# A two-block transformer layer on one core: the columns 1+ca as wide products, one pass for their stationary, and a new order of all operations

## The chip, the core and the metric

The kernel runs on one core of a Trainium2 chip. The core has five engines that run side by side, each in the order of its own instruction list: TensorE (PE, matrix products; PEld is its loading of the stationary operand), VectorE (DVE), ScalarE (ACT), GpSimd (POOL) and SyncE (SP), which here only issues DMAs. They wait for each other through semaphores. Products land in PSUM, eight banks of 128 x 512 floats; everything else lives in SBUF, which has 128 partitions.

The metric is the device time of one execution in microseconds (us). Of several executions the median counts.

## The reference

A layer with conditioning: six vectors of 512 numbers are made from `c`, and each of two blocks gets a shift, a scale and a gate.

```python
mod = (_silu(c) @ w_mod).reshape(c.shape[0], 6, 1, -1)
sa, ca, ga, sb, cb, gb = (mod[:, 0], mod[:, 1], mod[:, 2], mod[:, 3], mod[:, 4], mod[:, 5])
h = _layernorm(x, axis=-1) * (1 + ca) + sa
x = x + ga * _A_ref(h, A_wqkv, A_wo)                          # linear attention, 32 heads of 16
h = _layernorm(x, axis=-1) * (1 + cb) + sb
x = x + gb * _B_ref(h, B_w_in, B_w_sp, B_b_sp, B_w_out)       # gated MLP, mixing over positions
```

Block A: q, k, v = h @ wqkv; with phi(t) = (t+1 for t > 0, else exp(t)) + 1e-6 it sums phi(k) v and phi(k) over all positions for each head, multiplies by phi(q), divides, and applies wo. Block B: z = gelu(h @ w_in), split in two halves of 688; the second half is normalized and mixed over the positions by the 2048 x 2048 matrix w_sp, plus b_sp; the product of the halves goes through w_out. x is 2048 x 512. All is in 32-bit floats.

## The kernel before

The 2048 positions are 16 tiles of 128 rows, t = 0 to 15; the 512 features are four chunks of 128, kc = 0 to 3. Large products are made from operands split in a high part that is rounded for a faster matmul mode and a low part that holds the rest (`hi_lo`, `mm3`: three matmuls hi x hi, hi x lo, lo x hi, lines 110 to 112).

The program has two parts. Part one, in stages:

- **Head** (0 to about 38 us). The vector 1+ca is needed as a column for each chunk, because the layer norm's scale is folded into the weights. `silu` makes `sil` from `c`. `col_mm` (`cm`, line 196) multiplies each 128 x 128 block of w_mod[1], as stationary operand, by one column of `sil` and adds up into PSUM tile `pcol1`, 128 x 4. `col_end` (`ce1`, line 208) copies it to SBUF with 1 added. `mean_col` (`mc`, line 328) makes from it and from a tile `inv` filled with 1/512 a stationary `cbr` of four blocks, each with equal columns (1+ca)/512, in one ACT pass for each block. `mean_mm` (`mr`, line 334) multiplies `cbr` by w_k (j = 1) or w_q (j = 0): every row of the result `wm` is the mean to be taken out. `w_mid` (`wf`, line 338, on DVE) makes the folded weight w * (1+ca) - mean, `w_hi` (`qh`, ACT) and `w_lo` (`qd` on DVE, `qg` on POOL, line 345) split it into `wk` and `wq`. `load_m`, `load_wk` and `load_w` load w_mod, w_k and w_q; `dummy` (`du`, line 174) makes pairs of matmuls of ones that no one reads.
- **k, q and G** (to about 160 us). For each tile: the transposed x is split (`th`, `tl`, tile `ht`), products k (`kk`, `km`) and q (`qm`), phi on ACT and DVE, and `gm`, which adds phi(k)^T x into two PSUM tiles `g`.
- **The attention's small products** (to about 184 us): `kv` (tile `pkv`), mask and split into `kvh` (`kx`), then the four products with the gated w_o (`mm`, tile `pm`, one for each chunk; they share two PSUM tiles) and their splitting (`me`, tile `m`).
- **Output of block A and z** (to about 365 us). For each tile: q transposed (on PE, tile `tpp`, or by a DMA), the product with `m` (`wo`, tile `po`), x1, layer norm, transposing of h2 (tile `ht` again), the two z products with w_in (`z0`, `z1`, line 652: 24 matmuls each), gelu, and stores to DRAM. The last modulation row is made at the end (`mV`, `mS`, `mB`; tile `mod`).

Part two mixes over positions (`pp` for the first four row blocks, tile `Pq`; `pr` for the others by a scheme with fewer products, tile `P`, both line 930) and multiplies by w_out (`wm`, tile `pout`).

The order of the work is written out by hand: `ORDER` and `ORDER3` are lists of about 850 and 750 words, each an operation and its tile, in which every engine's instructions are recorded, and `SLOTS` says for each kind of buffer which of its places the next tile takes. A tile that takes a place must wait until the last reader of the tile before is done. All DMAs go through SP's one queue, in the order of the words. Line numbers here are those of the profile.

Of the kernel before, what the change touches and what calls it, by code (L numbers as in the profile page):

```python
# [26 lines left out]
def block_kernel(ctx: ExitStack, tc: tile.TileContext, x, x_t, w_qkv, w_o, w_in, w_sp, b_sp, w_out,  # L27
# [163 lines left out]
    def col_mm(m, kc):  # L191
        if m not in CP:
            CP[m] = ps("t", [P, KC], f"pcol{m}")
        for i in range(KC):
# [1 line left out]
            mm(CP[m][:, i:i + 1], RAW["mod", m, kc // 2][:, kc % 2, i * P:(i + 1) * P], sil[:, kc:kc + 1],
               start=n == 1, stop=n == KC * KC, skip_group_check=True)
# [8 lines left out]
    def col_end(key):  # L206
        COL[key] = const.tile([P, KC], F32, name=f"col{key}")
        nc.scalar.activation(COL[key], CP[key], AF.Copy, bias=1.0 if key == 1 else 0.0)
# [564 lines left out]
    def hx_lo(t):  # L773
# [21 lines left out]
        bh1 cr0 ce0 bp0 ly5 th5 lx2 s12 kr1 bh2 lx4 km2 kr2 qd0,1 by0 by1 by2 by3 bp3 qd0,3 qm0 bx1 bp1 tl5
        bh0 bp2 bb1 be1 bl0 ka0 qm1 qm2 qr0 qr1 lM2 ba1 ba2 ba3 lx5 s15 k20 bx0 km5 k40 bb0 s14 kh0 kl0 bl2
        ka2 gm0 be0 ly4 q12 th3 bh4 tl3 km3 lx3 qm3 lw2,0 k15 th4 s13 q22 q42 tl4 km4 qm4 bl1 kr3 ka1 mV2,0
        mV2,1 q13 k21 ly10 th10 bh3 bl3 k41 ks0 ks1 lw2,1 vh2 k22 k42 kh1 kl1 mS2 k25 kh2 bl4 k45 vh3 ly6 th6
        k14 k24 ks2 q14 q24 gm1 kl2 vh0 ly11 tl10 tl6 ly8 th11 th8 mB2 q44 lo0 lx6 s16 qm5 q15 ka3 k23 tl8 vl3
        ly9 km6 k16 k43 qm6 ks3 th9 tl9 tl11 lx9 s19 lx8 kh3 gm2 kl3 qa1 k44 ks4 q25 km8 s18 q16 bh9 kh4 gm3  # L800
        kl4 gm4 ly7 th7 tl7 bh6 vh1 lx7 ks5 k26 q45 km7 qm7 wg0 wx0 bl6 k46 lo1 wg2 bh8 bl8 kh6 kl6 q26 k18
        lx11 s17 q21 bl9 q46 kh5 ly15 th15 tl15 km9 bh5 wx2 ks6 bl5 k17 q41 q17 km11 ly12 k27 kl5 k47 k28 k48
        kh7 ly13 vl0 kl7 vl1 ks7 vl2 k19 th12 gm5 s111 lx15 km10 gm6 ly14 lx10 qa0 q27 tl12 ks8 wy0 qm10 s115
        q23 q43 bh7 kh8 vp0 q47 k111 s110 qm11 k29 kl8 k49 kh9 k110 k210 bl7 th13 q110 k211 k410 kh10 wg3 wx3
# [363 lines left out]
```

## Time and profile before

| what | value |
|---|---|
| median of 3 runs | 656.33 us (650.57 to 656.46) |
| the profiled execution: time, span of its instructions | 656.31 us, 654.2 us |
| PE busy | 629.8 us, 96% of the span |
| DVE busy | 506.2 us, 77% |
| ACT busy | 334.6 us, 51% |
| POOL busy | 226.6 us, 35% |
| 16 DMA engines, hardware queue | 53.5% |
| costliest matmuls | z, x768: 126.8 us; P, x576: 95.4 us; Pq, x384: 61.5 us |

Two other parts of the page show the span in 40 slices of 16.4 us and the chain of work that ended last. In a slice row each digit is a tenth of the slice's time.

```profile
PE   9999989999889899979999999999999999999998
DVE  0789999998779689864884579799698789884762
DMA  8235431344234555863473586642745767689862
PE 44%; DVE 15%; ACT 7%; issue 4%; DMA 3%; POOL 2%; SPq 0%; DVEq 0%; ACTq 0%; POOLq 0%
```

PE is nearly full everywhere. DVE is nearly full in slices 3 to 9, which are the k, q and G stage. DMA is fullest in the first slice. The chain's row adds up to 75% of the span, since its first piece starts at 161 us.

### The profile page before, as it was taken

To read this page: it belongs to the slowest core of one execution; us is meant where nothing else is said; L and a number is where in the kernel's file an instruction comes from. 1 tells how busy PE (TensorE), PEld (TensorE's weight loads), DVE (VectorE), ACT (ScalarE), POOL (GpSimd) and SP (SyncE) were. 2 spreads that over 40 slices of the span, in tenths; PEclk is the share of its full clock that TensorE was granted. 3 is DMA by queue.
4 is the path that set the end of the run, shared out by engine and by line. 5 is a ranking of instruction groups with operands and counts; after the bars stand their busy time and mean duration, and the time that the engine had idled before them with its cause. 6 is when DMAs were issued, how large, how long until landed. Compare 5 with 4: busy or idle time off the path is not lost.

```text
span 654.2 us, 9565 instructions
## 1 busy us (share of the span) xinstructions
PE 629.8 (96%) x3407; PEld 568.7 (87%) x3407; DVE 506.2 (77%) x910; ACT 334.6 (51%) x563; POOL 226.6 (35%) x186
## 2 busy tenths in 40 slices
PE   9999989999889899979999999999999999999998
PEld 9587777777778889879899999999999999998886
DVE  0789999998779689864884579799698789884762
ACT  1577775646446865457452564445444345443430
POOL 0562425625674566633524521140312221110000
PEclk9999999999999999989999999999999999999999
DMA  8235431344234555863473586642745767689862
GB/s 285 105 111 176 129 96 34 113 124 142 61 110 121 116 135 143 199 156 100 142 228 124 174 314 235 150 146 85 215 99 169 209 173 223 173 314 251 261 233 89
DMA packets 91310, 105.74 MB, mean 162 GB/s; under 512 B 57120, under 2 KB 57632, under 8 KB 91264
## 3 DMA queue, kind: packets, MB, share of 16 engines
q1 hardware_dynamic: 91264, 105.15, 53.5%
q8 instruction: 26, 0.43, 0.3%
q14 instruction: 20, 0.16, 0.1%
HBM read 66.07 MB, written 25.95 MB: 141 GB/s over the span
## 4 chain that ended last, share of the span: by engine, by line
PE 44%; DVE 15%; ACT 7%; issue 4%; DMA 3%; POOL 2%; SPq 0%; DVEq 0%; ACTq 0%; POOLq 0%
PE P L930 18%; PE Pq L930 9%; PE z L652 3%; PE pout L111 3%; PE pout L112 3%; PE pout L110 3%; DVE xpp L279 2%; DVE bst L250 2%; DVE xph L279 1%; POOL mv L255 1%; DVE h L262 1%; DMA wor<-in_w_out 1%; DVE ht L299 1%; DVE xr L628 1%; DVE h L261 1%
## 5 line engine op out<-in xcount | busy, mean ns | idle before, releaser
L652 PE MATMUL z<-win,ht 128*128 128x344 f32 x768 | 126.8, 324 | 7.3 <-DVE ht L299 2.8
L652 PEld LDWEIGHTS z<-win,ht 128*128 128x128 f32 x768 | 122.5, 191 | 11.4 <-DVE ht L299 3.5
L930 PE MATMUL P<-z,f 128*128 128x344 f32 x576 | 95.4, 320 | 1.1 <-DVE f L920 1.0
L930 PEld LDWEIGHTS P<-z,f 128*128 128x128 f32 x576 | 91.3, 188 | 1.7 <-DVE f L920 1.6
L920 POOL TENSOR_TENSOR f<-raw_wsp,f 128x512 fp32r<-128x512 f32 x24 | 37.5, 1575 | 122.9 <-ACT f L917 98.6
L255 POOL TENSOR_TENSOR mv<-ve,mhalf 128x1 f32<-128x1 f32 x48 | 37.5, 798 | 74.5 <-DVE ve L254 57.6
L930 PE MATMUL Pq<-z,wsp 128*128 128x344 f32 x384 | 61.5, 321 | 1.3 <-ACT mod L241 1.3
L930 PEld LDWEIGHTS Pq<-z,wsp 128*128 128x128 f32 x384 | 61.0, 188 | 1.6 <-ACT mod L241 1.5
L917 ACT ACTIVATE f<-sa 128x512 fp32r<-128x512 f32 x36 | 22.7, 630 | 50.2 <-DVE sa L907 12.5
L917 ACT ACTIVATE f<-raw_wsp 128x512 fp32r<-128x512 f32 x48 | 29.1, 625 | 21.4 <-PE P L930 9.4
L688 POOL TENSOR_TENSOR z<-zz,z 128x688 fp32r<-128x688 f32 x16 | 29.1, 1834 | 26.0 <-ACT z L685 26.0
L920 DVE TENSOR_TENSOR f<-sa,f 128x512 fp32r<-128x512 f32 x36 | 27.2, 758 | 9.1 <-ACT f L917 9.0
L111 PE MATMUL pout<-wout,ut 128*128 128x512 f32 (+1 forms) x85 | 32.5, 382 | 0.3 <-DVE wout L1050 0.3
L112 PE MATMUL pout<-wout,ut 128*128 128x512 f32 (+1 forms) x85 | 32.3, 380 | 0.0
L110 PE MATMUL pout<-wout,ut 128*128 128x512 f32 (+1 forms) x85 | 32.2, 379 | 0.0
L269 ACT COPY uca<-us 128x768 uint16<-128x768 uint16 x32 | 25.0, 828 | 13.8 <-DVE us L985 10.3
L472 POOL TENSOR_TENSOR pksum<-pksum,tk 128x512 f32<-128x512 f32 x15 | 22.7, 1511 | 26.3 <-DVE tk L444 19.5
L110 PE MATMUL kp<-wk,ht 128*128 128x512 f32 x64 | 26.0, 407 | 3.2 <-DVE tk L423 3.2
L1019 ACT ACTIVATE ut<-ur 128x384 fp32r<-128x384 f32 x32 | 15.5, 519 | 26.4 <-DMA ur<-ud 11.5
L269 ACT COPY xph<-h 128x512 uint16<-128x512 uint16 x28 | 15.9, 615 | 22.4 <-DVE h L262 17.8
L111 PE MATMUL kp<-wk,ht 128*128 128x512 f32 x64 | 25.4, 397 | 1.0 <-DVE wk L345 1.0
L112 PE MATMUL po<-m,pt 128*128 128x512 f32 x64 | 25.3, 396 | 0.6 <-POOL pt L299 0.6
(257 smaller groups left out, 1553.6 us busy)
## 6 DMA issues: line engine op xcount, KB each, us to landing
raw_wsp<-in_w_sp SPq DMA_DIRECT2D x32, 512.0 KB, 5.0
ud<-uca SPq DMA_DIRECT2D x16, 384.0 KB, 3.7
ur<-ud SPq DMA_DIRECT2D x16, 384.0 KB, 4.9
z1d<-z SPq DMA_DIRECT2D x16, 344.0 KB, 2.4
zd<-zz SPq DMA_DIRECT2D x16, 344.0 KB, 2.8
z1r<-z1d SPq DMA_DIRECT2D x16, 344.0 KB, 3.7
xt<-in_x_t SPq DMA_DIRECT2D x16, 256.0 KB, 2.8
x<-in_x SPq DMA_DIRECT2D x16, 256.0 KB, 2.8
```

The costliest lines, as they stand in the source:

```text
L110: mm(o, a_hi, b_hi, start=first, stop=False, **kw)
L111: mm(o, a_hi, b_lo, start=False, stop=False, **kw)
L112: mm(o, a_lo, b_hi, start=False, stop=last, **kw)
L255: nc.gpsimd.tensor_tensor(mv[:, 1:2], ve, mhalf, op=OP.pow)
L269: nc.scalar.copy(pl[:, h], v[:, :, h])
L279: copy(o[:, :, h], plt[:, h * n:(h + 1) * n].rearrange("p a b -> p (a b)"))
L472: nc.gpsimd.tensor_add(pksum, pksum, PK[t])
L652: mm(p[:, b, :HB], a[:, i, kc], win[h][:, j, kc, b * HB:(b + 1) * HB], start=kc == 0 and k == 0, stop=kc == KC - 1 and k == 2)
L688: nc.gpsimd.tensor_sub(Z2[t][:, 1], ZZ[t], f(Z2[t][:, 0]))
L917: nc.scalar.activation(SF[p, h, k][:, 0], s_src(p, h, k), AF.Copy)
L920: eng.tensor_sub(SF[p, h, k][:, 1], s_src(p, h, k), f(SF[p, h, k][:, 0]))
L930: mm(B[key][:, :HB], a[:, x_], b[:, y_], start=i == 1, stop=i == n)
```

## The change

Four things change.

1. `col_mm` multiplies by 128 equal columns of `sil` (a broadcast of one column) instead of one; the PSUM tile `pcol1` becomes 128 x 4 x 128, one bank.
2. `mean_col` makes the whole stationary `cbr` from that bank in one ACT pass, p/512 + 1/512. The tile `inv` and its fill go. `ce1` takes column 0 of each block and is no longer needed ahead of `cbr`.
3. On SP, w_k's fourth chunk is loaded before the second tile of x_t, and w_q's two loads stand together.
4. `ORDER`, `ORDER3` and `SLOTS` are new throughout. Six of eleven `du` and three of four `mc` words are gone; all other words are the same, in another order.

```diff
-    inv = sb("md", [P, P], F32R, "inv")
-    nc.gpsimd.memset(f(inv), 1.0 / D)
...
     def col_mm(m, kc):
         if m not in CP:
-            CP[m] = ps("t", [P, KC], f"pcol{m}")
+            CP[m] = ps("t", [P, KC, P], f"pcol{m}")
         for i in range(KC):
             n = NCOL[m] = NCOL.get(m, 0) + 1
-            mm(CP[m][:, i:i + 1], RAW["mod", m, kc // 2][:, kc % 2, i * P:(i + 1) * P], sil[:, kc:kc + 1],
-               start=n == 1, stop=n == KC * KC, skip_group_check=True)
+            mm(CP[m][:, i], RAW["mod", m, kc // 2][:, kc % 2, i * P:(i + 1) * P],
+               sil[:, kc:kc + 1].to_broadcast([P, P]), start=n == 1, stop=n == KC * KC, skip_group_check=True)
...
-        nc.scalar.activation(COL[key], CP[key], AF.Copy, bias=1.0 if key == 1 else 0.0)
+        p = CP[key][:, :, 0] if key == 1 else CP[key]
+        nc.scalar.activation(COL[key], p, AF.Copy, bias=1.0 if key == 1 else 0.0)
...
-    def mean_col(kc):
-        if "c" not in WC:
-            WC["c"] = sb("tb", [P, KC, P], F32, "cbr")
-        nc.scalar.activation(WC["c"][:, kc], f(inv), AF.Copy, scale=COL[1][:, kc:kc + 1])
+    def mean_col():
+        WC["c"] = sb("tb", [P, KC, P], F32, "cbr")
+        nc.scalar.activation(WC["c"], CP[1], AF.Copy, scale=1.0 / D, bias=1.0 / D)
...
-        lm1,0 si du1 du2 du3 du4 du5 cm1,0 lm1,1 du6 cm1,1 lm1,2 du7 cm1,2 lm1,3 lk1 lk0 du8 cm1,3 ce1 mc0 ly1
+        si lm1,0 du1 du2 du3 du4 cm1,0 lm1,1 cm1,1 lm1,2 cm1,2 lm1,3 cm1,3 mc lk0 lk1 ly1 th1 tl1 lk2 lk3 du5
```

Three places of the new order, as the recorded instruction lists show them (line, operation, output<-inputs, size; numbers in names only tell tiles apart).

The head, on PE, before:

```order
L174 MATMUL warm<-ones 128x128 x10
L196 MATMUL pcol_187<-sil,raw_mod_0_170 128x1 x4
L174 MATMUL warm<-ones 128x128 x2
L196 MATMUL pcol_187<-sil,raw_mod_0_170 128x1 x4
L174 MATMUL warm<-ones 128x128 x2
L196 MATMUL pcol_187<-sil,raw_mod_1_199 128x1 x4
```

And now:

```order
L172 MATMUL warm<-ones 128x128 x8
L194 MATMUL pcol_183<-sil,raw_mod_0_173 128x128 x8
L194 MATMUL pcol_183<-sil,raw_mod_1_193 128x128 x8
L172 MATMUL warm<-ones 128x128 x2
L332 MATMUL wm_219<-raw_qkv_0_206,cbr 128x512 x2
```

The dummies between the columns are gone, and the sixteen column products stand together. The same place on SP, before:

```order
L156 DMA raw_qkv_0_208<-in_w_qkv 128x512 x2
L150 DMA xt_221<-in_x_t 128x512
L156 DMA raw_qkv_1_226<-in_w_qkv 128x512
L150 DMA xt_231<-in_x_t 128x512
L156 DMA raw_qkv_1_226<-in_w_qkv 128x512
L144 DMA raw_qkv_0_250<-in_w_qkv 128x1024
L156 DMA raw_mod_0_255<-in_w_mod 128x512
L144 DMA raw_qkv_1_257<-in_w_qkv 128x1024
```

And now:

```order
L154 DMA raw_qkv_0_206<-in_w_qkv 128x512 x2
L148 DMA xt_209<-in_x_t 128x512
L154 DMA raw_qkv_1_214<-in_w_qkv 128x512 x2
L148 DMA xt_221<-in_x_t 128x512
L154 DMA raw_mod_0_226<-in_w_mod 128x512
L142 DMA raw_qkv_0_230<-in_w_qkv 128x1024
L142 DMA raw_qkv_1_232<-in_w_qkv 128x1024
```

The fourth chunk of w_k moved ahead of the second x_t tile, and the two loads of w_q no longer have a load of w_mod between them.

The products with the gated w_o, on PE, before; of each product only the first of its three rows is shown:

```order
L306 MATMUL tpp_1742<-ident,pq_473 128x128 x4
...
L110 MATMUL pm_0_1753<-wog_920,kvh 128x512
...
L110 MATMUL pm_0_1753<-wog_1311,kvh 128x512
...
L110 MATMUL pm_2_1769<-wog_977,kvh 128x512
...
L110 MATMUL pm_2_1769<-wog_1163,kvh 128x512
```

And now:

```order
L305 MATMUL tpp_1700<-ident,pq_430 128x128 x4
...
L110 MATMUL pm_0_1716<-wog_1061,kvh 128x512
...
L110 MATMUL pm_2_1722<-wog_1267,kvh 128x512
...
L110 MATMUL qp_1729<-wq_161,ht_1017 128x512
...
L110 MATMUL pm_0_1716<-wog_1224,kvh 128x512
...
L110 MATMUL pm_2_1722<-wog_1232,kvh 128x512
```

The q product of tile 14, twelve matmuls, stood ahead of all four; it now stands between the first pair, one in each PSUM tile, and the second.

The border of the two programs, on PE, before:

```order
L652 MATMUL z_14_3664<-win_1440,ht_14_3460 128x344 x24
L238 MATMUL pmod_3701<-yh_3595,ones 128x512
L239 MATMUL pmod_3701<-yl_3596,ones 128x512
L930 MATMUL Pq_0_3767<-z_0_2574,wsp_0_3350 128x344 x3
L930 MATMUL Pq_1_3771<-z_0_2574,wsp_0_3350 128x344 x3
```

And now:

```order
L237 MATMUL pmod_3658<-yh_3590,ones 128x512
L238 MATMUL pmod_3658<-yl_3591,ones 128x512
L650 MATMUL z_15_3663<-win_1707,ht_15_3475 128x344 x24
L928 MATMUL Pq_0_3749<-z_0_2534,wsp_0_3621 128x344 x3
L928 MATMUL Pq_1_3753<-z_0_2534,wsp_0_3621 128x344 x3
```

The last modulation row's products moved ahead of the last z product, and the first mixing product is that of row block 1, whose PSUM banks are others than those of block 0.

More of the change, by code (lines that the diff above doesn't have):

```diff
@@ L795, in block_kernel @@
[L795 to L804, printed above, removed]
@@ L825, in block_kernel @@
[L825 to L827 removed]
+        si lm1,0 du1 du2 du3 du4 cm1,0 lm1,1 cm1,1 lm1,2 cm1,2 lm1,3 cm1,3 mc lk0 lk1 ly1 th1 tl1 lk2 lk3 du5
+        mr1,0 ly0 th0 tl0 lm0,0 mr1,1 mr1,2 lw0,0 lw0,1 ce1 mr1,3 wf1,3 qh1,3 qg1,3 mr0,0 yp0,0 lm0,2 wf1,1
@@ new lines, in block_kernel @@
+        qm14 lX5 wl0,3 wh1,1 wl1,0 me0 me2 ae0 at1 ae1 mm1 me1 wh1,2 wl1,1 mm3 me3 q114 at3 ae3 wl1,2 d24 wo0
+        x10 wo3 x13 wh1,3 wl1,3 h20 wo1 w02 q214 ap4 d25 d17 ht0 w12 he0 za0 zb0 x12 ap5 am4 ah4 al4 q215 h22
+        hp2 q213 h23 am5 z00 wo4 ah5 al5 q413 g10 wo5 lX4 x11 hm2 h21 ht1 hh2 hl2 z12 g20 hp3 d110 d16 lX7 d27
+        zl0 he1 z01 g22 lX9 d19 q414 lX6 d26 x14 ap7 ap6 hm3 h24 hh3 g11 hp4 hl3 d210 x15 h25 lX12 z02 g12 zn0
+        z13 g23 hm4 hh4 z11 am6 am7 hp5 ah7 ah6 q415 d115 hl4 z04 d18 lX10 zl2 d29 g21 al7 d28 zl3 d215 z14
@@ new lines, in block_kernel @@
+        g24 hm5 hh5 hl5 d112 ap10 zl4 al6 ap8 zn2 g14 zl1 ap9 wo7 x17 zn3 zp3 z15 h27 hp7 am10 am8 zn1 d212
+        lX8 ah10 al10 z05 g15 ah8 al8 zp1 zh0 am9 ah9 wo6 x16 d111 zp0 hm7 hh7 z03 zn4 zp4 g13 hl7 wo8 al9
+        d211 ap11 g25 z07 x18 ap12 h26 hp6 d113 zl5 zn5 h28 zh1 am11 zh2 zo2 hp8 d213 z17 ah11 al11 zh4 wo9
+        x19 hm6 hh6 hm8 zp2 hh8 wo10 lX11 g17 h29 hp9 hl8 x110 g27 hl6 wo11 ap15 h210 lX13 am12 ah12 al12 hm9
+        hh9 z08 g18 zl7 zo1 hp10 zp5 z16 g26 ap13 hl9 zn7 d114 d214 z09 g19 z06 z19 g16 x111 zp7 zo4 hm10 hh10
@@ L828, in block_kernel @@
+        g214 aH1,0 aL1,0 aH0,0 zh9 zo9 z014 g114 mB5 z115 g215 aL0,0
     """
@@ new lines, in block_kernel @@
+        td2 ts5 tl0,4 lh4,0 aH1,2 aL1,2 td5 th5,5 tl5,5 th0,6 aH2,2 ss2,0,3 aL1,3 fh2,0,1 pp0,3 lz0 th2,6
+        ss2,0,1 ts1 pp0,2 th0,5 aL2,2 pp1,3 td1 th1,7 ce0,0 th1,5 ce0,1 um0 aL2,3 fl2,0,1 ts4 th2,4 pp1,2 lz1
+        tl2,6 up0 th0,7 tl0,7 ts6 lh3,1 tl1,5 tl1,7 th1,6 td4 ux0 th1,4 fh2,0,4 fg2,0,4 td6 tl1,4 pp2,2
+        fh2,0,7 ce1,0 fl2,0,7 lz2 th6,6 ce1,1 tl6,6 aH3,3 th4,6 ss2,0,2 pr2,0,1 um1 tl1,6 ug0 lh4,1 pp2,3
+        tl2,4 aH3,2 lh5,1 ce2,0 fh2,0,6 fl2,0,6 fh2,0,2 ce2,1 um2 uq0 aG3,3 tl0,6 tl4,6 tl0,5 pp3,1 th3,7
@@ new lines, in block_kernel @@
+        fl4,1,5 pr4,1,5 fh4,1,3 fg4,0,4 ug5 uq5 fl4,0,5 cd4,2 fl4,1,3 um7 pr4,0,5 fh4,0,6 fl4,0,6 pr4,0,6
+        lh11,0 ss4,0,4 ss5,0,3 ux6 fl4,0,7 fh4,0,3 pr4,0,7 fl4,0,3 up7 pr4,0,4 fh5,0,7 fl5,0,7 cs4,6 cs4,5
+        pr5,0,7 cs4,7 lz8 lh10,1 fh5,1,1 lh11,1 fh5,0,4 fh5,1,2 pr4,0,3 fg5,1,2 pr5,1,2 fh5,1,4 ug6 uq6
+        ss5,0,1 ss5,0,2 fh5,0,6 fg5,0,4 pr5,0,4 cd4,4 ss5,1,3 ux7 fl5,1,1 ss5,1,1 ss5,1,2 pr4,1,3 pr5,1,1
+        fh5,0,5 fh5,1,7 ug7 fh5,1,6 uq7 fl5,0,5 fh5,1,5 fl5,1,6 ss5,1,4 pr5,1,6 fl5,0,6 ss5,0,4 fl5,1,5
@@ L1132, in block_kernel @@
+        cs7,0 ur8 um14 ug12 uq12 uh1 ul1 wm1 ug13 lx12 lx6 uh8 uh4 ul4 ur6 uh6 uq13 lx1 ur5 lz15 lx7 ur12 ot0
+        ot1 wm4 ul6 up14 ux14 uh5 ul5 um15 up15 ux15 wm6 ul8 ur7 wm8 ot2 ur9 ot3 uh12 ul12 wm5 ug15 uh7 uq15
+        uh11 ur10 ul7 wm7 uh10 ot4 ug14 uq14 ul11 ot5 ur13 ot6 ur15 ot7 lx11 wm11 uh9 ul9 wm9 lx14 ul10 wm10
+        lx9 uh13 ul13 ot8 ur14 uh14 ot9 ot10 wm12 ot11 wm13 ul14 wm14 uh15 ul15 ot12 ot13 wm15,0,256 ot14
+        wm15,256,512 ot15,0,256 ot15,256,512
     """
```

161 lines of the change are left out of this document (72 added, 89 removed).

## The prediction

> **What bounds the kernel now.** I read the shares of the span first, then the table of windows, the timeline of the first 40 us, and last the waits of PE with the timeline around the long ones. The first row is from the page's part 1; the others are windows (from:to, length, then busy time and count of PE, PEld, DVE, ACT and POOL, the granted clock, the DMA share, GB/s).
>
> ```profile
> PE 629.8 (96%) x3407; PEld 568.7 (87%) x3407; DVE 506.2 (77%) x910; ACT 334.6 (51%) x563; POOL 226.6 (35%) x186
> 27.00:60.00 33.00, 33.00 (x152) 26.89 (x151) 30.73 (x59) 24.23 (x41) 17.49 (x16) 1.00 0.37 122
> 60.00:100.00 40.00, 38.22 (x164) 30.34 (x163) 39.17 (x64) 29.74 (x49) 14.01 (x11) 1.00 0.37 111
> 190.00:290.00 100.00, 92.50 (x516) 83.58 (x515) 86.56 (x168) 62.05 (x104) 60.10 (x52) 1.00 0.58 145
> 365.00:528.00 163.00, 161.72 (x1023) 161.08 (x1023) 131.63 (x229) 77.58 (x137) 41.60 (x27) 1.00 0.61 188
> ```
>
> PE idles for only 654.2 - 629.8 = 24.4 us. From 27 to 100 us DVE is as full as PE (39.17 of 40), so a gain before 27 us lasts only if DVE starts earlier too. From 365 to 528 us nothing but matmuls counts. The widest loose stretch is 190 to 290 us, with 7.5 us idle. But busy does not mean quick: in the first 20 us PE counts as busy while it runs at half speed, as the timeline shows (start, duration, engine, line, operation, what waited for what).
>
> ```profile
> 0.99 4.64 PE L174 MATMUL warm<-ones 128*128 128x128 f32 x20 [0.99 <-POOL ones L120]
> 7.77 1.83 PEld L196 LDWEIGHTS pcol<-sil,raw_mod 128*128 128x128 f32 x8
> 12.89 1.83 PEld L196 LDWEIGHTS pcol<-sil,raw_mod 128*128 128x128 f32 x8
> 14.84 0.17 ACT L208 ACTIVATE col<-pcol 128x4 f32<-128x4 f32 x1 [12.23 <-PE pcol L196]
> 15.66 9.33 PE L334 MATMUL wm<-raw_qkv,cbr 128*128 128x512 f32 x16
> 18.29 0.34 PEld L334 LDWEIGHTS wm<-raw_qkv,cbr 128*128 128x128 f32 x1 [0.52 <-issue]
> 20.53 0.19 PEld L334 LDWEIGHTS wm<-raw_qkv,cbr 128*128 128x128 f32 x1 [0.24 <-issue]
> 21.59 2.72 DVE L338 SCALAR_TENSOR_TENSOR wf<-raw_qkv,col,wm 128x512 f32<-128x512 f32 x4 [3.36 <-PE wm L334]
> 26.20 0.50 PE L111 MATMUL kp<-wk,ht 128*128 128x512 f32 x1 [0.98 <-DVE wk L345]
> 37.34 0.68 DVE L345 TENSOR_TENSOR wq<-wf,wq 128x512 fp32r<-128x512 f32 x1
> 183.35 0.87 PE tpp L306 x8
> ```
>
> The same weight load takes 0.34 us at 18.29 and 0.19 at 20.53, so the clock opens between them, although the windows print a granted clock of 1.00 from the start. The last row, from the chain of waits, gives the open pitch of 128 columns: 0.87/8 = 0.109 us. The shut one is 4.64/20 = 0.232. A load of PE that runs one column wide keeps it busy but, by these rows, did not open the clock between 5 and 15 us; wide matmuls without a break did, some 5 us after they began. (Each matmul of 32-bit floats appears twice, so 16 products are 32 instructions.)
>
> **The head, part by part.** Removed: six of eleven pairs of dummies, three ACT passes, and the GpSimd fill of `inv`, which cost nothing since GpSimd waits until 23 us for its first real work. The order of PE and of SP there stands with the change: the dummies between the columns are gone and the columns are one wide run; on SP the fourth chunk of w_k changes place with the second tile of x_t.
>
> Landing times bound this, one pair of rows each for the four chunks of w_mod, the four of w_k, the first two tiles of x_t and the first of x (issue times, then microseconds to landing). Last come a copy of 128x512 out of PSUM, the price of the single pass that makes the stationary, and a cast of a w_k chunk.
>
> ```profile
> L156 SPq DMA_DIRECT2D raw_mod<-in_w_mod x4: 417/428/432, 1.2 to 2.6; - x4
> DMA to landing us min/median/max: 3.3/4.7/5.0
> ...
> L156 SPq DMA_DIRECT2D raw_qkv<-in_w_qkv x4: 328/432/642, 3.1 to 6.3; - x4
> DMA to landing us min/median/max: 6.7/6.8/7.3
> ...
> L150 SPq DMA_DIRECT2D xt<-in_x_t x2: 431/527/623, 4.0 to 5.2; - x2
> DMA to landing us min/median/max: 7.1/7.2/7.3
> ...
> L136 SPq DMA_DIRECT2D x<-in_x x1: 328/328/328, 11.1 to 11.1; - x1
> DMA to landing us min/median/max: 6.6/6.6/6.6
> ...
> 159.06 0.60 ACT L707 ACTIVATE zrep<-pz 128x512 f32<-128x512 f32 x1 [1.37 <-PE pz L703]
> 22.37 2.60 ACT L342 ACTIVATE wk<-wf 128x512 fp32r<-128x512 f32 x4 [4.94 <-DVE wf L338]
> ```
>
> Dummies: 16 x 0.232 = 3.7, from 0.99 to 4.7. Columns: a wide one costs the 0.232 of a dummy, a narrow one 1.83/8 = 0.229, so width is free. The clock's opening is not shown for this mix. The bounds are 5.6 us (the 4.64 us of dummies did not quite do it) and never before `wm`; I take 7, nearest the 5 us that `wm` needed. Then 10 columns run shut and 22 open: 7.0 + 22 x 0.109 = 9.4, against 14.7 before. All of w_mod is there by 2.6 + 5.0 = 7.6. The single pass (0.60 and two starts) puts `wm` at 10.3. But the fourth chunk of w_k, now in the place of an x_t tile issued at 5.2, lands at 5.2 + 7.3 = 12.5, so the last `wm` pair ends near 13.6. `ce1`, moved behind both `ht` casts on ACT, waits for the tile of x_t that now lands at 13.1, and ends at 14.0. So `wf` starts at 14.2, not 21.59: 7.4 earlier. From here DVE sets the pace (the first k product waits for its low part at 26.20). It has the work that took it from 21.59 to 37.34 + 0.68 = 38.0 before the last part of w_q is done. Two of its steps now wait: the low part of chunk 0 stands right behind its `wf` and needs ACT's cast first (0.65, the mean of the four in the last row), and the cast of chunk 2 stands on ACT behind `ht` of tile 3, whose load is the next after some 17 of 256 KB; the 17th, the x tile above, landed at 11.1 + 6.6 = 17.7. I estimate 1.4 us for both. **Head: -6.0 us**, bounds -7.4 (no such wait) and -2.5 (clock shut until `wm`: columns end at 12.1, eight `wm` take the 5.7 us they took before, `wf` starts at 18.9).
>
> The Trainium skill, page "TensorE: Matmul & The Clock Gate", Part 1 (the HAM clock gate), says the gate opens after about 3.4 us of sustained activity, in a free-running window. By that rule the clock would open here between 4.4 and 7.8 us, and the sum would stay, as w_k's landing sets `wm`. The rows agree in part: 4.64 us of dummies did not open it, which a window out of step with the start allows. The same rule would also let the old kernel open early wherever the window happens to fit its dummies; that would shrink the gain there, not lengthen the new time. No trace here shows such an execution.
>
> From rows alone: one of three runs took 650.57, 5.7 less than the profiled 656.31, about what an early clock would give. The median, 656.33, is like the profiled run (span 654.2 and 2.1 outside it), so the sum stands against the median as it is.
>
> **The products with w_o.** Waits of PE (what waited, for what, total, times, longest), then the timeline there:
>
> ```profile
> PE pm L110 <- DVE m L130: 2.9, 1, 2.9
> PE Pq L930 <- ACT mod L241: 1.3, 1, 1.3
> ...
> 171.11 0.22 PE L723 MATMUL pkv<-gh,wv 128*128 128x128 f32 x1
> 171.17 0.45 PE L110 MATMUL qp<-wq,ht 128*128 128x512 f32 x1
> 175.50 0.69 DVE L130 TENSOR_TENSOR kvh<-kvm,kvh 128x512 fp32r<-128x512 f32 x1 [0.76 <-ACT kvh L129]
> 176.78 0.60 PE L306 MATMUL tpp<-ident,pq 128*128 128x128 f32 x4
> 177.14 0.48 PE L110 MATMUL pm<-wog,kvh 128*128 128x512 f32 x1
> 182.39 0.50 PE L110 MATMUL pm<-wog,kvh 128*128 128x512 f32 x1 [2.91 <-DVE m L130]
> ```
>
> The four `pm` products share two tiles, and the last waits until DVE has read the third. In the new order, shown with the change, one q product (12 matmuls, 2.8 us) moved from before the four to between the pairs. It covers the reads, so the 2.9 us go. What is late next is `kvh`: after the last `pkv` it took until 176.2, 5.0 us, and the cover falls from 5.9 to 3.1 us; its low part is needed half a microsecond into `pm`, so about 1.3 us of wait appears. **-1.6 us**, bounds -2.9 and 0.
>
> **The border of the two programs.** The wait on `mod` is 1.3 us at 366 us, where the first `Pq` reuses a bank that ACT is still reading. As shown with the change, a whole z product (24 matmuls) now lies between, and row block 1, in other banks, goes first. **-1.3 us**, bounds -1.3 and 0; behind it PE alone counts.
>
> **All else.** Each remaining operation is moved but none is added, so DVE's, ACT's and the DMA queue's totals stay. In 190 to 290 us the new order could take away up to the 7.5 us or add as much; I take 0. The load of the last modulation moves from 159 us to the late z products:
>
> ```profile
> L144 SPq DMA_DIRECT2D raw_mod<-in_w_mod x2: 327/331/335, 158.6 to 159.1; - x2
> ```
>
> It no longer holds two of the eight `s4` buffers all that time. Behind it on SP stand transposes and stores of the z stage, but SP comes to it after the store of x tile 12, which needs later products than the last readers of its two buffers: no wait seen. Sum: 656.3 - 6.0 - 1.6 - 1.3 = 647.4.
>
> **Rivals.** (a) The clock stays shut until `wm`: -2.5 instead of -6.0, 650.9. The 4.64 us of dummies speak for it; that columns now fill PE without a gap speaks against. (b) The new order takes half of the loose 7.5 us away: 643.6. For it: of z tiles 2 to 15, nine had their first product right behind the step that completes its operand, now five. (c, d) One such operand is late. The price is a row of before:
>
> ```profile
> 289.86 5.42 PE L652 MATMUL z<-win,ht 128*128 128x344 f32 x23 [2.30 <-DVE ht L299]
> 280.00:300.00 20.00, 17.04 (x96) 16.28 (x95) 13.40 (x28) 10.39 (x18) 6.75 (x7) 0.91 0.50 128
> ```
>
> PE waited 2.3 us there, and the window lost 0.09 x 20 = 1.8 us of clock: 4.1 together. One such wait gives 651.5 (c). From three of the five on, the kernel is slower: 647.4 + 12.3 = 659.7 (d), and with four 663.8. DVE's 86.56 of 100 us speaks for such waits, the fewer tight places against.
>
> **How the numbers follow.** Chances: forecast 0.48, with a range of its own from 644.5 to 649.5; (a) 0.19; (b) 0.10; (c) 0.11; (d) 0.12, half of it beyond three waits. A measurement can tell about 1% from no change, here 6.6 us. Below 649.8 lie the forecast and (b): faster 0.58. Within 1% lie (a), (c) and half of (d): 0.36. Slower 0.06. The range, 642.5 to 655.5, takes in (a), (b) and (c), and leaves (d) and the extremes out.
>
> **What would show it.** Right: `pcol` instructions near 0.11 us from 7 us on; weight loads of `wm` at 0.19 from the first; `wf` near 14 us and the last part of w_q near 32; `pm` without a wait over 1.5 us; no wait for `mod` at the border. Wrong: `wm` loads at 0.34, `wf` after 18 us, or new PE waits over 2 us in the z products.

## The result, and the profile after

The changed kernel takes 626.63 us (median of 4 runs, 624.06 to 628.32) where the kernel before, beside it, takes 654.33 (650.57 to 656.46): ratio 0.9579, 95% interval 0.9515 to 0.9644. The prediction was 647.4, with a range from 642.5 to 655.5: the direction was right, the size was not, by 20.8 us. The profiled execution after took 625.56 us, 623.5 of them its span; 30.7 us are to be explained between the two traces.

First the stages, before and then after, cut where the first product of each kind starts (head, k/q/G, small products, output of A and z, first row blocks; columns as in the prediction's windows: busy time and count of PE, PEld, DVE, ACT, POOL, granted clock, DMA share, GB/s).

```profile
0.00:24.40 24.40, 23.41 (x84) 18.44 (x85) 4.58 (x10) 5.92 (x13) 1.93 (x10) 1.00 0.72 258
24.40:158.40 134.00, 128.99 (x561) 102.43 (x560) 126.22 (x206) 91.50 (x148) 62.67 (x49) 1.00 0.34 104
158.40:184.00 25.60, 21.23 (x116) 17.57 (x114) 17.17 (x29) 11.72 (x23) 17.86 (x14) 1.00 0.37 117
184.00:364.70 180.70, 172.31 (x974) 159.09 (x972) 137.95 (x272) 101.32 (x165) 92.13 (x79) 0.99 0.52 138
364.70:411.90 47.20, 45.95 (x289) 45.66 (x288) 34.65 (x69) 24.60 (x44) 14.05 (x10) 1.00 0.78 259
```

```profile
PE 615.2 (99%) x3383; PEld 559.2 (90%) x3383; DVE 483.8 (78%) x910; ACT 328.9 (53%) x556; POOL 221.8 (36%) x185
...
0.00:18.00 18.00, 14.96 (x69) 10.50 (x69) 5.40 (x10) 6.47 (x12) 2.98 (x9) 1.00 0.85 292
18.00:145.90 127.90, 127.13 (x553) 101.71 (x552) 113.48 (x205) 89.78 (x146) 57.96 (x48) 1.00 0.38 120
145.90:167.90 22.00, 21.36 (x115) 17.42 (x114) 17.03 (x30) 12.39 (x24) 16.61 (x13) 1.00 0.16 45
167.90:334.70 166.80, 166.80 (x974) 158.31 (x973) 128.25 (x272) 97.24 (x162) 93.10 (x81) 1.00 0.61 166
334.70:380.40 45.70, 45.70 (x290) 45.70 (x290) 32.93 (x64) 21.91 (x38) 13.03 (x9) 1.00 0.68 233
```

The head gives 6.4 us, k/q/G 6.1, the small products 3.6, the z stage 13.9, the first row blocks 1.5; what follows takes 0.9 more. In the z stage PE now never idles. DVE's 910 instructions last 22.4 us less in all, although none was removed. The waits of PE (what, for what, total, times, longest), the largest of before that the prediction did not show, and then all those of after over 0.2 us:

```profile
PE kp L110 <- DVE tk L423: 3.2, 2, 1.6
PE z L652 <- DVE ht L299: 2.8, 2, 2.3
PE z L652 <- ACT zz L663: 2.1, 2, 1.1
PE z L652 <- ACT z L657: 1.9, 3, 0.7
PE pkv L721 <- DVE gh L130: 1.5, 1, 1.5
```

```profile
PE wm L332 <- DMA raw_qkv<-in_w_qkv: 1.6, 1, 1.6
PE warm L172 <- POOL ones L120: 1.0, 1, 1.0
PE qp L111 <- DVE wq L343: 0.6, 1, 0.6
PE pout L111 <- DVE wout L1048: 0.6, 1, 0.6
PE pkv L719 <- DVE gh L128: 0.5, 1, 0.5
```

A finer count takes the distance from each matmul's start to the next, less the median of its kind (by the tiles it writes and reads), and adds these up: 27.0 us before, 4.3 after. Half of the 22.7 us between lies in the z products (11.5). These 22.7 us, 24 fewer dummy records of 0.213 us (5.1) and 32 column records at 0.112 instead of 0.213 us (3.2) make the 30.7 to within 0.3. The 3.2 are the clock as well: in e7, where it was open, eight records of the narrow columns took 0.95 us, against 1.71 in before. So about 26 us are waits that are gone and the clock that was open; only 5 are work taken away. Last the head, on PE and DVE:

```profile
4.68 4.16 PE L194 MATMUL pcol<-sil,raw_mod 128*128 128x128 f32 x32 [0.19 <-DMA raw_mod<-in_w_mod]
9.53 3.70 PE L332 MATMUL wm<-raw_qkv,cbr 128*128 128x512 f32 x8 [0.24 <-ACT cbr L326]
14.85 3.67 PE L332 MATMUL wm<-raw_qkv,cbr 128*128 128x512 f32 x8 [1.62 <-DMA raw_qkv<-in_w_qkv]
...
13.71 2.72 DVE L336 SCALAR_TENSOR_TENSOR wf<-raw_qkv,col,wm 128x512 f32<-128x512 f32 x4
30.17 0.68 DVE L343 TENSOR_TENSOR wq<-wf,wq 128x512 fp32r<-128x512 f32 x1
```

`wf` starts at 13.71 (predicted 14.2, before 21.59) and the last part of w_q is done at 30.85 (predicted 32, before 38.0).

### The profile page after: what moved, and what is told of

It reads as the page before. It is cut to its first block, busy times and chain, and to the rows that moved or that the text cites. A ratio compares the mean times of both kernels' runs of the same rounds, so it can differ in the third digit from the quotient of the medians.

```text
span 623.5 us, 9515 instructions
## 1 busy us (share of the span) xinstructions
PE 615.2 (99%) x3383; PEld 559.2 (90%) x3383; DVE 483.8 (78%) x910; ACT 328.9 (53%) x556; POOL 221.8 (36%) x185
## 4 chain that ended last, share of the span: by engine, by line
PE 80%; DMA 8%; DVE 7%; issue 2%; ACT 1%; SPq 0%; ACTq 0%; DVEq 0%
PE z L650 19%; PE P L928 17%; PE Pq L928 10%; PE pout L111 3%; PE pout L112 3%; PE pout L110 3%; PE po L110 2%; PE po L111 2%; PE po L112 2%; DMA raw_qkv<-in_w_qkv 2%; PE g L112 2%; PE qp L111 2%; PE qp L112 2%; PE g L110 2%; PE g L111 2%; PE qp L110 2%
## 5 line engine op out<-in xcount | busy, mean ns | idle before, releaser
L650 PE MATMUL z<-win,ht 128*128 128x344 f32 x768 | 122.7, 320 | 0.0
L918 POOL TENSOR_TENSOR f<-raw_wsp,f 128x512 fp32r<-128x512 f32 x24 | 35.9, 1509 | 148.4 <-ACT f L915 128.5
L915 ACT ACTIVATE f<-raw_wsp 128x512 fp32r<-128x512 f32 x48 | 29.3, 626 | 32.3 <-DMA raw_wsp<-in_w_sp 12.9
L470 POOL TENSOR_TENSOR pksum<-pksum,tk 128x512 f32<-128x512 f32 x15 | 22.8, 1517 | 49.4 <-DVE tk L442 45.3
L915 ACT ACTIVATE f<-sa 128x512 fp32r<-128x512 f32 x36 | 22.5, 629 | 33.3 <-DVE sa L908 7.8
L1017 ACT ACTIVATE ut<-ur 128x384 fp32r<-128x384 f32 x32 | 15.2, 517 | 31.1 <-DMA ur<-ud 14.2
L111 PE MATMUL qp<-wq,ht 128*128 128x512 f32 x64 | 25.3, 395 | 0.6 <-DVE wq L343 0.6
L110 PE MATMUL kp<-wk,ht 128*128 128x512 f32 x64 | 25.9, 404 | 0.0
L579 POOL TENSOR_TENSOR prod<-pq,zrep 128x512 f32<-128x512 f32 x16 | 21.4, 1342 | 11.7 <-ACT zrep L705 4.2
L112 PE MATMUL g<-pkhl,hhl 128*128 128x512 f32 x64 | 25.3, 395 | 0.2 <-DVE hhl L394 0.2
```

Source lines behind the costliest of these rows:

```text
L110: mm(o, a_hi, b_hi, start=first, stop=False, **kw)
L111: mm(o, a_hi, b_lo, start=False, stop=False, **kw)
L112: mm(o, a_lo, b_hi, start=False, stop=last, **kw)
L470: nc.gpsimd.tensor_add(pksum, pksum, PK[t])
L579: nc.gpsimd.tensor_mul(pr, PQ[t], KV["z"])
L650: mm(p[:, b, :HB], a[:, i, kc], win[h][:, j, kc, b * HB:(b + 1) * HB], start=kc == 0 and k == 0, stop=kc == KC - 1 and k == 2)
```

## The experiments

Lengths by stage, in us to about 0.1, from the profiled execution of each kernel, cut at the first product of each kind as above:

| kernel | head | k/q/G | small | z | Pq | P | pout | span |
|---|---|---|---|---|---|---|---|---|
| before | 24.4 | 134.0 | 25.6 | 180.7 | 47.2 | 175.4 | 66.9 | 654.2 |
| after | 18.0 | 127.9 | 22.0 | 166.8 | 45.7 | 175.8 | 67.3 | 623.5 |
| e1_head_only | 17.8 | 133.3 | 27.0 | 182.5 | 47.2 | 176.8 | 66.8 | 651.4 |
| e2_narrow_no_dummies | 18.9 | 133.9 | 26.1 | 182.5 | 47.3 | 176.2 | 67.5 | 652.4 |
| e3_before_no_switch | 24.7 | 134.0 | 25.6 | 179.5 | 47.3 | 176.3 | 67.4 | 654.8 |
| e4_after_switch | 17.7 | 128.2 | 22.1 | 169.2 | 45.7 | 174.9 | 66.4 | 624.2 |
| h1_new_kqg | 18.0 | 127.8 | 26.3 | 182.7 | 45.8 | 184.1 | 66.9 | 651.6 |
| h1b_same_slots | 17.5 | 128.3 | 25.7 | 183.4 | 45.8 | 174.6 | 66.8 | 642.1 |
| h2_new_z | 24.7 | 133.8 | 23.1 | 166.7 | 45.7 | 176.2 | 66.7 | 636.9 |
| e5_quiet_pool | 18.9 | 128.5 | 27.1 | 175.5 | 47.3 | 174.8 | 66.8 | 638.9 |
| e6_after_narrow | 19.5 | 128.7 | 22.0 | 166.8 | 45.7 | 175.1 | 67.1 | 624.9 |
| e7_moves | 20.5 | 134.0 | 22.4 | 183.3 | 45.7 | 174.4 | 66.3 | 646.6 |
| e8_moves_quiet | 18.7 | 128.6 | 22.5 | 179.1 | 45.8 | 176.6 | 66.5 | 637.8 |
| e9_after_quiet | 17.8 | 127.6 | 22.1 | 166.7 | 45.8 | 176.3 | 67.1 | 623.4 |
| e10_before_extra | 24.5 | 133.9 | 25.7 | 191.0 | 47.3 | 174.6 | 66.4 | 663.4 |
| e11_after_extra | 17.7 | 127.9 | 22.0 | 174.4 | 45.7 | 174.7 | 66.6 | 629.0 |

### Which part of the change earns what

The new head alone, in the old order (e1):

```diff
-        lm1,0 si du1 du2 du3 du4 du5 cm1,0 lm1,1 du6 cm1,1 lm1,2 du7 cm1,2 lm1,3 lk1 lk0 du8 cm1,3 ce1 mc0 ly1
-        mc1 mc3 mc2 lk2 ...
+        lm1,0 si du1 du2 du3 du4 cm1,0 lm1,1 cm1,1 lm1,2 cm1,2 lm1,3 lk1 lk0 cm1,3 mc ce1 ly1 lk2 ...
```

> The old kernel with the new head alone: wide columns, the stationary in one pass, no dummies between the columns; the order of everything else, the loads too, is the old one. Theory H (the head is worth what its own stage shows): wf starts near 14 us as in the new kernel, the first kp near 18 to 19, and all later stages keep their old lengths (134 us from the first kp to the first pz, 181 from the first po to the first Pq): 5 to 8 us less than before, 648 to 651. Rival S (the earlier head gives DVE the lead that also takes the waits of the k, q and G stage away): that stage falls from 134 towards 128 and the time to 643 or less.

Measured: 652.98 us (10 runs; before beside it 654.65), ratio 0.9955, interval 0.9928 to 0.9981. Its trace starts the k products 6.6 us earlier and ends 2.8 earlier. It lost 2.4 us where the wait of 2.91 us for `m` made the clock close (from 174.1 to 180.9 us in the clock's record), the rest in the z stage and in P. So a head ahead of the old order is worth about 3 us (1.2 to 4.7 by the interval), and the other 25 lie elsewhere. Rival S is out: the k, q and G stage keeps 133.3 us.

Next, splices at the first `kv` word: the new order up to there and the old one behind it (h1), and the reverse, with the old head (h2).

```
h1: after's code,  ORDER = after up to kv0 + rest of before, ORDER3 = before's
h2: before's code, ORDER = before up to kv0 + rest of after, ORDER3 = after's
(ten words stand ahead of kv0 in one order only; they go by the order behind the splice)
```

> The kernel after with its own order up to the first product of the value sum (kv0) and the old order from there to the end; slots are given anew behind that point. Order theory, stage by stage: the saving lies where the new order lies. First k product at about 18 us (before 24.4), first pkv 7 to 8.5 us after the end of a k/q/G stage of 128 us (before 134), then the old lengths: z stage about 181 us, so 654.3 - 6.4 - 6.1 = 641 to 643 us, and PE waits over 0.25 us sum to 26.85 - 8 = about 18 us. Rival, slack handed on: with everything ahead of time at kv0 the old z order has its inputs earlier and also loses waits: 630 to 637 us. Rival, clock: one more closing of the clock (3.4 us at half) gives back 1.7 us or more: 643 to 645.

> The kernel before (old head, old columns) with its own order up to kv0 and the new order from there to the end. Order theory, stage by stage: head and k/q/G keep 24.4 and 134 us, the stages from the first pkv on take those of after: 654.3 - (31 - 12.5) = about 636 us; PE waits from 158 us on under 3 us. Rival, the saving needs the early half: the new z order finds its inputs as late as the old one did and waits again: 645 us or more.

Measured: h1 654.54 us (10 runs), ratio 1.001, 0.9985 to 1.0036; h2 639.6 us (4 runs), ratio 0.977, 0.9709 to 0.9831. h2 is as the theory by stages has it: the z stage takes 166.7 us although it starts as late as in the old kernel. h1 ends the k, q and G stage 12.6 us early as expected, but gives 8.7 us back in P, whose order it shares with the kernel before. What differs there is the buffers: 24 tiles behind the splice had been given other ones. So the same splice was run with the old buffers, renamed (h1b).

```
h1:  behind the splice 24 of 587 tiles in another buffer than before's
h1b: behind the splice every tile in before's buffer, up to one renaming per pool
```

> The same splice as the first (new head and new order up to kv0, old order behind it), with every tile behind the splice in the buffer that it has in the kernel before, up to one renaming of the buffers per pool. Stage theory: it reaches kv0 12.6 us early and keeps that up to the clock closings of the old z order (1.7 us each after the 2.5 to 3 us waits): 641 to 645 us, second program's 32 products of 24 in 175 to 177 us as before. Rival, the gain is given back behind the border by the old order itself: 650 to 655 again with a stage of 180 us or more there.

Measured: 645.3 us (4 runs), ratio 0.9855, 0.9813 to 0.9896; P takes 174.6 us again. The two halves, 10.1 us (h1b) and 14.6 us (h2) on the medians, make 24.7 of the 27.7. The 3.0 left over are no more than the intervals of the two ratios allow (some 2.7 and 4 us to either side). Two closings of the clock in h1b (169.9 to 173.3 and 279.1 to 282.5 us) may be part of it; in the kernel after it never closes within the span.

### The head: columns and dummies

Narrow columns in the kernel after (e6), and the kernel before without the three dummies between its columns (e2):

```diff
# e6, on after
-            mm(CP[m][:, i], ..., sil[:, kc:kc + 1].to_broadcast([P, P]), ...)
+            mm(CP[m][:, i:i + 1], ..., sil[:, kc:kc + 1], ...)
# e2, on before
-        cm1,0 lm1,1 du6 cm1,1 lm1,2 du7 cm1,2 lm1,3 lk1 lk0 du8 cm1,3
+        cm1,0 lm1,1 cm1,1 lm1,2 cm1,2 lm1,3 lk1 lk0 cm1,3
```

> The kernel after with the columns 1+ca of width 1 again (32 narrow products); one-pass stationary, loads and order stay. If the wide columns are what opens the clock: clock shut until about wm, first k product 2 to 6 us later, and since the new order has no waits to swallow it the end is as much later: 629 to 633 us. If the dummies and the weights' arrival set the head: first k product within 1 us of 18.0, time 626 to 628.

> The old kernel with narrow columns, and without the three pairs of dummies between them. If the wide columns open the clock (theory W), the clock here stays shut through the columns: weight loads of wm still take 0.34 us, and wf starts only about 2 us earlier, near 19.5. If the dummies in between were all that cost time (rival), wf starts near 15 us and the time falls by 6.

Measured: e6 627.97 us (4 runs), 1.3 above the kernel after, and in its trace 1.5 us later at the first k product and 1.4 at the end. That lies between the two expectations: the head is later by more than 1 us, the time is not 629. With no waits behind it, the new order carries what the head gains to the end. e2, one run: 654.55 us, with a head of 18.9 us instead of 24.4. Neither of its expectations holds, and the dummies are not the reason: e5 and e8, which have all of them, show 18.9 and 18.7. The clock's record tells the difference. With the old head it first opens at 20.2 to 20.7 us (before, e3, h2, e10; heads of 24.4 to 24.7) or at 3.9 to 5.2, and then closes again for 3.4 to 6.8 us while the one-column products run (e2, e5, e7, e8; 18.7 to 20.5). With wide columns it opens at 4.1 to 6.9 us in all six executions that have the record, and no head shows it closing: 17.5 to 18.0 us. So the 6.4 us of the two traces shown is the gain over the late kind; over the early kind it is 0.7 to 3.

### ACT's table loads

The old order has exps of q between gelus, hence four more table loads of 1.28 us; the new one doesn't. Taken out of before (e3; the exp of q tiles 14 and 15 is replaced by a copy, so their rows differ), and put into after (e4, two tiny exps between gelus):

```diff
# e3, on before
-        nc.scalar.activation(EK[key], EK[key], AF.Exp, scale=-1.0)
+        nc.scalar.activation(EK[key], EK[key], AF.Copy if key in (("q", 14), ("q", 15)) else AF.Exp, scale=-1.0)
# e4, on after
+    def tiny_exp(k):
+        nc.scalar.activation(sm([P, KC], "tx"), cT, AF.Exp, scale=-1.0)
-        ... z12 g20 hp3 d110 d16 lX7 d27 zl0 he1 z01 g22 lX9 ...
+        ... z12 g20 tx0 hp3 d110 d16 lX7 d27 zl0 he1 z01 g22 tx1 lX9 ...
```

> The old kernel with the exponential of q tiles 14 and 15 replaced by a copy (same size and engine, so their rows of the result are left wrong): ACT loads its tables twice instead of six times, 5.1 us of ACT less between 205 and 224 us. Theory T (these loads are a large part of what the z stage lost): PE's waits between 207 and 234 us go and the stage from first po to first Pq falls by 4 to 6 us, to 175 to 177. Rival D (the stage hangs on DVE's chain whatever ACT does): it falls by 1.5 us or less.

> The new kernel with two tiny exponentials (128x4) on ACT, one after the second gelu and one after the third, which bring back four table loads at the old places and nothing else. Theory T: the stage from first po to first Pq grows from 166.8 us by 4 to 6, and the time to 630 to 632. Rival: the new order has slack there and hides them: 1.5 us or less.

Measured: e3 654.24 us (10 runs), ratio 0.9982, 0.9948 to 1.0016; e4 627.47 us (4 runs), 0.8 above the kernel after. The z stage shortens by 1.2 us in e3 and grows by 2.4 in e4. So e3 is as the rival has it, and e4 lies between. In e3 the clock happened to close for 6.83 us (286.9 to 293.7) where the kernel before lost 3.41, about 1.2 us more, so the loads may be worth some 2.4 us there as well. They are a small part of the stage's 13.9 us, and none that can be measured at the end.

### Vector work behind POOL

This place of the old order stands ahead of one of the two waits for `tk` (POOL, DVE, PE):

```profile
89.46 1.38 POOL L472 TENSOR_TENSOR pksum<-pksum,tk 128x512 f32<-128x512 f32 x1
...
89.60 1.78 DVE L404 TENSOR_TENSOR ht<-xt,ht 128x512 fp32r<-128x512 f32 x1
...
92.77 0.50 PE L110 MATMUL kp<-wk,ht 128*128 128x512 f32 x1 [1.65 <-DVE tk L423]
```

The same `ht` subtraction takes 0.68 us where POOL is idle. Here it starts 0.14 us after POOL's sum and ends 0.54 after it, as if it had stood still meanwhile: it shares 1.24 us with the sum and is 1.10 us longer than alone. `tk`, two instructions behind it, is late by as much, and k's bank with it. The Trainium skill, "SBUF — State Buffer", section "SBUF: two separate sides", says that the two engines hold one port pair by an exclusive lock for a whole instruction, where the vector instruction has two inputs in SBUF and POOL's reads SBUF. These rows agree, to the 0.14 us by which 1.10 falls short of 1.24. POOL's instructions that nothing on PE's path waits for were made small, in before (e5) and in after (e9). This leaves the sum over k features and the low parts of z2 out of the result.

```diff
-            nc.gpsimd.tensor_add(pksum, pksum, PK[t])
+            nc.gpsimd.tensor_add(pksum[:, 0:1], pksum[:, 0:1], PK[t][:, 0:1])
...
-        nc.gpsimd.tensor_sub(Z2[t][:, 1], ZZ[t], f(Z2[t][:, 0]))
+        nc.gpsimd.memset(f(Z2[t][:, 1]), 0.0)
```

> The kernel before with POOL made quieter: the 15 sums of k features take one column instead of 512, and the 16 low parts of z2 are a memset to zero (so the running sum and the low parts of z2 are left out of the result); nothing that PE waits for in these stages needs either. POOL theory (vector instructions stretched while POOL runs make the late operands): DVE busy falls by 10 us or more, the waits of 1.81 us at 92.8 (tk behind an ht of 1.78 us) and 2.46 us at 289.9 (ht of 2.06 us) go, PE waits fall from 26.9 to under 20 us, the time by 5 to 10 us to 645 to 649. Rival, order theory (leads of the order too short whatever the durations): DVE shorter, but waits still 22 us or more and the time 650 to 654.

> The kernel after with the same quieter POOL (the running sum of k features and the low parts of z2 left out). If the new order has already taken the stretched vector instructions off the path: DVE busy shorter by 10 us and the time the same, 625 to 627.5. If they still cost it what they cost the old order: 616 to 620.

Measured: e5 643.88 us (4 runs), ratio 0.9863, 0.9796 to 0.993; e9 623.94 us (4 runs), ratio 0.9529, 0.9482 to 0.9575, which overlaps the interval of after. In e5 the two waits for `tk` shrink from 3.2 us to 0.3 and the longest one for `ht` from 2.3 to 0.9; its time is a little below the forecast of the POOL theory. In e9 the time hardly moves, as the first expectation has it. The k/q/G and z windows of e5, then of e9:

```profile
18.90:147.40 128.50, 127.24 (x560) 102.86 (x559) 113.97 (x205) 91.18 (x148) 44.13 (x49) 1.00 0.35 114
...
174.50:350.00 175.50, 169.84 (x973) 157.93 (x971) 130.38 (x274) 100.82 (x165) 78.89 (x79) 1.00 0.52 142
```

```profile
17.80:145.40 127.60, 126.96 (x552) 101.76 (x551) 112.15 (x205) 89.50 (x146) 40.68 (x48) 1.00 0.39 120
...
167.50:334.20 166.70, 166.70 (x973) 158.21 (x971) 123.14 (x275) 97.00 (x162) 80.42 (x81) 1.00 0.61 166
```

In k/q/G, quieting POOL takes 12.3 us off DVE (126.22 to 113.97) in the old order and 5.5 us off the stage, nearly what the new order gives (6.1). In the new order it takes 1.3 us off DVE (113.48 to 112.15) and nothing off the stage: the same sums, 22.8 us of POOL, stand there beside vector work that they don't hold up. So in k/q/G vector work held up by POOL accounts for 5.5 of the 6.1 us. In the z stage quieting POOL gives 5.2 of the 13.9 us, one closing of the clock included.

The traces of before and after show the same without leaving anything out. Take each DVE instruction's length above the fastest tenth of its kind (line and tiles), and sort by whether it overlaps a POOL instruction:

| kernel | beside POOL, all | k/q/G | z | not beside POOL, all |
|---|---|---|---|---|
| before | 66.6 | 19.0 | 23.6 | 7.1 |
| after | 42.7 | 6.7 | 14.0 | 7.1 |

So DVE's fall is all beside POOL. In the z stage it is 9.6 us by this count, and the stage's DVE work is 9.7 us shorter.

### The z stage: single words, or the lead of the whole

The z waits of the old order were read so: an engine holds PE's operand or bank behind a word that itself waits. In e7 the words of this diff were moved; in e8 POOL was made quiet as well (the same sums left out):

```diff
-  mm2 me2 mm3          +  mm2 mm3 me2
-  he1 zn0 zp0 d26 z12 g22 zl2 q215     +  he1 d26 z12 g22 zn0 zp0 zl2     (q215 behind q214)
-  am6 hm4 hh4 h25 z13 g23              +  am6 z13 g23 hm4 hh4 h25
-  hh8 h29 hp9 hl8 z08                  +  hh8 hl8 h29 hp9 z08
-  z16 d214 ah12 hm9 al12 lX13 h211 lX12 hh9 hl9 z19 g18
+  z16 g18 d214 ah12 hm9 hh9 hl9 al12 lX13 h211 lX12 z19
-  g215 z014 ... zo1 mB5                +  g215 mB5 z014 ... zo1
```

> The kernel before with eleven words of the old order moved a few places, nothing else: the last vector matrix product ahead of the evacuation it needn't follow (mm3), two exp next to each other (q215), the norm of z2 of tile 0 behind a gelu (zn0, zp0), a transposed tile's split behind a gelu (hm4, hh4, h25), two low parts ahead of another tile's normalisation (hl8, hl9 before h29, h211), a gelu ahead of a division and a split (g18), the sum over mod 5 one product earlier (mB5). Queue theory (an in-order engine holds the operand or the bank that PE wants behind a word that waits): the waits at 182.4 (3.07), 220.3 (1.16), 224.9 (0.72), 233.8 (1.27), 278.7 (0.64), 286.7 (0.82), 289.9 (2.46) and 366.6 (1.42) go or halve, and the closing of the clock at 289.9 (1.7) with them: 7 to 13 us, 641 to 647 us. Rival, engines short of time (POOL and vector work take what they take, and the wait shows up at the next operand): under 4 us, 650 to 654.

> The eleven moved words and the quieter POOL together (the running sum of k features and the low parts of z2 left out). If the two causes are separate, their gains add: 643.9 less 6 to 10 us, 633 to 638. If they are the same waits, 641 to 645.

Measured: e7 651.95 us (10 runs), ratio 0.9958, 0.9927 to 0.999; e8 640.01 us (4 runs), ratio 0.9784, 0.9741 to 0.9828. The words outside the z stage did what they should: small products 25.6 to 22.4 us, first row blocks 47.3 to 45.7. Inside it most of the named waits went and others came; the stage is 2.6 us longer. The time is as the rival has it. e8 lies between its two expectations, and its z stage is 3.6 us longer than e5's: there too the moves gained nothing. PE's longest z waits in e7:

```profile
PE z L645 <- ACT ht L122: 2.7, 1, 2.7
PE z L645 <- ACT zz L656: 2.4, 1, 2.4
PE z L645 <- ACT z L650: 2.1, 2, 1.4
```

So moving these words did not mend the z stage. What the new order has throughout shows when one measures, in the traces, how long before its use each operand is there: from the end of the vector instruction that writes the low part of tile `ht` to the first matmul that reads it (16 places), and from the end of a gelu to the first matmul into the bank that it frees (30 places).

| kernel | low parts: under 0.3 us, least, median | gelus: under 0.3 us, least, median |
|---|---|---|
| before | 5, 0.06, 1.3 | 7, 0.05, 1.6 |
| e7_moves | 5, 0.06, 1.2 | 3, 0.05, 1.8 |
| e5_quiet_pool | 5, 0.06, 1.3 | 6, 0.05, 2.4 |
| after | 0, 0.50, 2.1 | 0, 0.42, 2.2 |
| h2_new_z | 0, 0.50, 2.1 | 0, 0.50, 2.2 |
| e4_after_switch | 1, 0.05, 1.6 | 1, 0.05, 1.8 |
| e10_before_extra | 4, 0.05, 1.1 | 7, 0.05, 1.5 |
| e11_after_extra | 3, 0.06, 0.9 | 7, 0.05, 1.5 |

The old order has leads up to 9.6 us (low parts) and 12.9 us (gelus) beside a dozen of none; the new one's reach 4.4 and 5.6, and none is under 0.4. But the number of tight places alone does not give the length of the stage: e7 has eight and takes 183.3 us, e5 eleven and 175.5. To see whether this lead is what pays, the first of two vector instructions of each tile's second layer norm was done twice from the same inputs, in before (e10) and in after (e11).

```diff
         nc.vector.scalar_tensor_tensor(h, src, MEAN[key], scale, op0=OP.subtract, op1=OP.mult)
+        nc.vector.scalar_tensor_tensor(h, src, MEAN[key], scale, op0=OP.subtract, op1=OP.mult)
```

> The kernel before with the first of the two vector instructions of each tile's normalisation ahead of the z products done twice (16 more instructions of 0.68 to 0.75 us, about 12 us of DVE, all in the 181 us of the z stage; the result is the same). Lead theory: the low parts of five tiles and seven gelus reach PE 0.05 us ahead of use here, so DVE's extra time goes straight to PE at each such place and to those behind it: z stage 4 to 10 us longer, 658 to 665 us. Rival, capacity: DVE is busy 83% of this stage, has room for 12 us, and the time moves by under 2 us.

> The kernel after with the same 16 instructions more. Lead theory: every low part and gelu of the z stage stands 0.4 us or more ahead of use, 2.1 us in the middle, and one instruction of 0.7 us a tile is taken from that: z stage 0 to 3 us longer, 626 to 630 us, at most a third of what the kernel before loses. Rival, capacity: as much longer as the kernel before, or more, since the stage is 14 us shorter and DVE fuller.

Measured: e10 665.19 us (4 runs; before beside it 654.16), 11.0 more than before, ratio 1.0164, 1.0116 to 1.0213. e11 630.56 us (4 runs), 3.9 more than after, ratio to before 0.964, 0.959 to 0.969. The z windows of e10 and of e11:

```profile
184.10:375.10 191.00, 177.18 (x972) 163.02 (x971) 150.03 (x287) 101.38 (x165) 92.69 (x79) 0.96 0.47 131
```

```profile
167.60:342.00 174.40, 169.87 (x974) 157.63 (x973) 146.60 (x288) 97.16 (x162) 93.19 (x81) 1.00 0.58 159
```

The lead theory forecast too little for both. The old order's stage grows by 10.3 us (4 to 10 were expected), about 4 of them clock: it closes four times, before once, and each closing costs 1.0 to 1.5 us by the distances between matmuls. The new order's stage grows by 7.6 us where 0 to 3 were expected, all of it waits, since no stretch of its matmuls runs at half speed. Without the clock the two are hit much alike, by some 6 and by 7.6 us. At the end the new order loses 3.9 us on the medians, 5.5 between the two traces; that is a third to a half of the old one's 11.0. The capacity rival is out for the old order, which lost far more than 2 us, and for the new one it holds only if the clock is left out.

DVE is also hit harder in the new order, 128.25 to 146.60 against 137.95 to 150.03: 6.7 us of the 18.4 are instructions beside POOL that became longer (14.0 to 20.7 by the count above; in the old order 23.6 and 23.5). With the same 16 instructions more, ten of its 46 places stand at none.

So this is shown: the new order of the second half alone makes the stage 14 us shorter (h2), its DVE work is held up less by POOL, and its leads are even. That a long lead saves it from more vector work is not shown. If the 9.6 us of DVE that it saves beside POOL are worth to it what quieting POOL was worth to the old order, they make about 6 of the 13.9 us, by estimate (the same count falls by 8.1 us in e5, for 5.2 of the stage). What makes the other 8 stays open.

## Why the prediction was wrong

- **The head, -6.0: the mechanism and the path were right** (`wf` 13.71, w_q 30.85; the first k product 6.4 us earlier). The size was right only against the one profiled execution, which the sum took as typical. Four of the eight traces with the old, narrow columns opened the clock early (e2, e5, e7, e8), and e1 shows what the head is worth over many runs, 0.45%, some 3 us. The remark that the old kernel could open early, for which no trace stood then, was the right doubt. The clock opened at 4.1 us, not 7, and as said this changed little, since w_k's four products ended at 13.23 (predicted 13.6).
- **The products with w_o, -1.6: right mechanism, under-sized.** The wait of 2.9 us went; the wait for `kvh` that was put at 1.3 us came to 0.28. With the shorter wait for `gh` the stage gave 3.6.
- **The border, -1.3: right.** No wait; the stage gave 1.5.
- **All else, 0: this step failed.** It said: "Each remaining operation is moved but none is added, so DVE's, ACT's and the DMA queue's totals stay. In 190 to 290 us the new order could take away up to the 7.5 us or add as much; I take 0." The totals did not stay. DVE's fell from 506.2 to 483.8 us with the same instructions, because an instruction's length depends on what POOL does beside it (e5, and the count beside POOL, 66.6 to 42.7 us). And the looseness was counted in one window. By stages, PE stood idle for 5.0 us in k/q/G and 8.4 in the z stage; after, for 0.8 and none. Its busy time there fell besides, by 1.9 and 5.5 us with the same matmuls (172.31 to 166.80 in the z stage), which holds the closed clock (1.3 us) and pauses that count as busy. Together these are the 6.1 and 13.9 us. The splices show that both come with the order of their own half. In k/q/G the step failed by the vector work that POOL held up; in the z stage that explains less than half, and the rest of the cause is open.
- **Rivals.** (b), that the order takes waits away, was the true one, with a chance of 0.10 and capped at 3.8 us by the same window. (c) and (d), single late operands, did not occur: none of the waits after is in a z product. Counting tight places (nine against five; eight against four, if only words that stand next to each other count) pointed the right way, and was used only to weigh a rival. The price of a late operand, 2.3 + 1.8 us, had the clock a little too dear: by the distances between matmuls that closing cost 1.3.
